# Other durations and the shared port in an attention planner, and float64 weights decoded by a multiplication

## The chip, the cores and the metric

The kernel runs on one core of one Trainium2 chip. The metric is the time of one execution on the device in microseconds. Its engines are named as the profile names them: PE (TensorE, matrix products), DVE (VectorE), ACT (ScalarE), POOL (GpSimd) and SP, whose queue issues the DMAs.

## The reference

Three layers follow one another: attention in which a query sees only the keys that fall in the same hash bucket, a dense layer pair with the Mish activation, and eight experts with a gate that is normalised by eight Sinkhorn rounds.

```python
q_bits = (np.einsum('bhsd,dk->bhsk', q, proj) > 0).astype(np.int64)   # 16 heads, 768 tokens, 64 wide
...
mask = q_bucket[:, :, :, None] == k_bucket[:, :, None, :]
scores = np.where(mask, scale * np.matmul(q, k.transpose(0, 1, 3, 2)), -1000000000.0)
scores = scores - np.max(scores, axis=-1, keepdims=True)
attn = np.exp(scores) / (np.sum(np.exp(scores), axis=-1, keepdims=True) + 1e-09)
x = np.matmul(attn, v)                                                # -> 1536 tokens x 512
...
h = x @ w_in                                                          # 512 x 2048, w_in and w_out are float64
x = (h * np.tanh(np.log1p(np.exp(h)))) @ w_out
...
for e in range(8):                                                    # P: the normalised gate
    out += P[:, e:e + 1] * (np.maximum(x @ w1[e], 0.0) @ w2[e])
```

`w_in` and `w_out` reach the kernel as 64-bit words and are turned into pairs of 32-bit parts on the chip.

## The kernel before

Attention comes first (to 291.3 us of the profiled execution), then the dense layer and the experts, which are one long row of matmuls.

Attention works on 32 units `u`, half a head's 384 queries each, and six blocks `c` of 128 keys. Scores are computed twice. `s_mm` (L379) makes them with the queries on the partitions, rounded, only for the row maxima: `s_max` (L393, DVE, read from PSUM; one buffer, tag `s`), `cols` (L398, L399, DVE) gathers three maxima and flags into columns, `rows_mm` (L412, PE) transposes them, `rows_cp` (L421, ACT) copies them out, and three small DMAs (`rows_move`) put them under the queries. `st_mm` (L429, L430) then makes the exact scores with the keys on the partitions and the maximum already subtracted; `st_exp` (L435, ACT) takes the exponential into one of five buffers `p`. Blocks 0, 1, 3 and 4 are split into a rounded part (`split_hi`, the tile `ph`, L438) and a rest (`split_lo`, the tile `plo`, L441, POOL) for three fast products; blocks 2 and 5 go into one slow product as they are. Both are `av_mm` (L479). `av_out` (L487 on DVE, L489 on ACT) reads the result out, `norm` (L498 to L510, and casts and subtractions on L438 and L441) divides.

For each head, `prep_hi` (L300, ACT) and `prep_lo` (the tile `lo`, L441) split the loaded queries and keys, `bits_mm` and `bits_cmp` (L326 to L338) make the hash bits, `split_v` (the tiles `vh`, `vl`) splits the values, and `vsum_red` (L348, DVE) sums them.

Beside all this, eight half chunks of the 64-bit weights are loaded and decoded while attention runs (`decode`, L132 to L165). A half chunk is 128 x 512 numbers, each a low and a high 32-bit word. Parts 0, 1 and 3 to 6 work on the high word: the sign is kept aside (L135), the absolute value is taken (L137 on DVE or L139 on ACT), it is clamped (L143), its exponent is moved into the 32-bit place (L147), the sign comes back (L151), and the power of two is cut out (L155). Part 2 (L141, ACT) turns the low word into a float, part 7 (L157, POOL) scales it and part 8 (L159) adds the two. `weight_hi` and `weight_lo` (L171, L176) split the finished chunk. The other 24 half chunks are decoded beside the dense layer by the same function, in an order written out in the code.

What sets the order inside attention is a list scheduler that runs while the program is built. Every step is a task with an engine (or a choice of two), a cost in us, a due time in steps and the tasks it waits for. In each round the planner takes, of the tasks whose predecessors are placed, the one with the smallest start plus 0.012 times its due time on each engine, and of these the earliest start. `free[e]` is when an engine is free, `ends[k]` when a task's readers may start. So a cost changes the order in which instructions stand in each engine's queue; at run time each queue is worked in that order, with semaphores for the data.

```python
task("P1.8|D.87" if h else "D.5|", 0, due - 14.0 + 1 if h else -50, prep_lo, h, i, after=[his[i], *moved])
task("D", 0.87, due + 2 * t + 0.5, s_max, u, t, after=[nm(s_mm, u, t)] + [nm(cols, u - 2)] * (t == 0 and u > 1))
...
free[e] = start + cost
ends[k] = start + cost + LAT[e]
```

Of the kernel before, what the change touches and what calls it, by code (L numbers as in the profile page):

```python
# [22 lines left out]
E = 8  # L23
# [16 lines left out]
RECEIPT = 0.95  # L40
# [6 lines left out]
LOW64 = float(2.0 ** -15)  # L47
HIGH64 = float(122880.0)
# [9 lines left out]
def lsh_attention_moe_kernel(  # L58
# [72 lines left out]
    def decode(i, j, part, e="A"):  # L131
        t = staged[i, j]  # L132
        lw, hw = t[:, :, 0], t[:, :, 1]
        if part == 0:
            nc.vector.tensor_scalar(out=sgn[j], in0=hw, scalar1=-0x80000000, scalar2=None, op0=ALU.bitwise_and)  # L135
        elif part == 1 and e == "D":
            nc.vector.tensor_scalar(out=hw, in0=hw, scalar1=0x7FFFFFFF, scalar2=None, op0=ALU.bitwise_and)  # L137
        elif part == 1:
            nc.scalar.activation(f32(hw), f32(hw), AF.Abs)  # L139
        elif part == 2:  # L140
            nc.scalar.activation(f32(lw), lw.bitcast(U32), AF.Copy, scale=2.0 ** -52)  # L141
        elif part == 3:
            nc.vector.tensor_scalar(  # L143
                out=f32(hw), in0=f32(hw), scalar1=LOW64, scalar2=HIGH64, op0=ALU.max, op1=ALU.min
            )
        elif part == 4:
            nc.vector.tensor_scalar(  # L147
                out=hw, in0=hw, scalar1=0x38000000, scalar2=3, op0=ALU.bitwise_xor, op1=ALU.logical_shift_left
            )
        elif part == 5:  # L150
            nc.vector.scalar_tensor_tensor(  # L151
                out=hw, in0=hw, scalar=0x7FFFFFFF, in1=sgn[j], op0=ALU.bitwise_and, op1=ALU.bitwise_or
            )
        elif part == 6:
            nc.vector.tensor_scalar(out=sgn[j], in0=hw, scalar1=-0x800000, scalar2=None, op0=ALU.bitwise_and)  # L155
        elif part == 7:
# [26 lines left out]
    def attention():  # L183
        with ExitStack() as a:
# [334 lines left out]
            def task(engine, cost, due, f, *args, after=(), lag=None, ring=None, frees=None):  # L519
                tasks[f.__name__, *args] = (engine, cost, due, f, args, list(after), lag, ring, frees)  # L520

            LAT = {"E": 0.2, "A": 0.12, "D": 0.1, "P": 0.12, "Q": 0.0}
# [11 lines left out]
            task("D", 1.4, -99, clear_start)  # L534
            task("E", 5.0, -99, warm_up, after=[nm(clear_start)])
            task("A", 1.5, -99, load_table, after=[nm(clear_start)])
            for j in range(4):
                task("Q", 0.6, (-98, -97, -26, 20)[j], load_const, j, lag=0.1)
            task("D", 0.55, -8, proj_parts, after=[nm(clear_start), nm(load_const, 0)])
            for c in range(2):  # L540
                task("D", 0.2, -2, count_rows, c, after=[nm(load_const, 2), nm(clear_start)])
            task("D", 0.3, 20, gate_parts, after=[nm(load_const, 3)])
            for i in range(NS):
                for n, kind in enumerate(("sq", "bk", "one")):
                    e = "D" if (kind, i) in FAST else "P"
                    task(e, 0.7, -8.5 + 3 * i + n / 4, clear, kind, i, after=[nm(clear, "bk", i)] * (n == 2))
            for i in range(2):
                for kind in ("vt", "vh", "vl"):
                    task("P", 0.35, -3 + 2 * i, clear, kind, i)


            for h in range(NH):
# [5 lines left out]
                task("Q", 0.6 if h else 1.2, due - 24 if h else -99, load_qk, h, lag=1.65 if h else 1.3,  # L558
# [3 lines left out]
                for i in range(len(halves(h))):  # L562
                    task("A", 0.75 if h else 0.38, due - 14.0 if h else -50, prep_hi, h, i,
                         after=[nm(load_qk, h), *moved] + [nm(bits_mm, h - 1, j) for j in range(2) if h])
                    task("P1.8|D.87" if h else "D.5|", 0, due - 14.0 + 1 if h else -50, prep_lo, h, i, after=[his[i], *moved])
# [739 lines left out]
```

## Time and profile before

| | us |
|---|---|
| median of 3 runs | 1586.91 (1584.88 to 1586.96) |
| the profiled execution | 1585.57 |
| its span, first to last instruction | 1583.8 |
| attention, to the first matmul of the dense layer | 291.3 |
| PE busy, whole span | 1549.1 (98%) |
| in attention, busy: PE, DVE, POOL, ACT | 261.8, 251.8, 204.0, 186.3 |

A busy time is the sum of the spans in which an engine had an instruction under way. On PE these overlap and their ends are modelled, so the number of matmuls in a stretch says more than the busy time. On DVE and POOL an instruction's span includes time in which it stood still.

### The profile page before, as it was taken

The page shows a single profiled execution, that of the slowest core. Times are in us where ns is not written, and L with a number is a line of the kernel's source. Part 1 is how long each engine was busy: PE and PEld are TensorE (multiplying, and loading weights), DVE is VectorE, ACT ScalarE, POOL GpSimd, SP SyncE. Part 2 cuts the span into 40 slices and gives each one's busy share as a digit, 9 for nine tenths or more (in the row PEclk, how much of TensorE's full clock was granted, in tenths as well). Part 3 has the DMA queues.
Part 4 walks back from the last instruction along what each step waited for, and adds up shares of the span by engine and source line. Part 5 has one row for each costly group of instructions (what it writes and reads, how often), then busy time and mean ns, then how long its engine had stood idle before and what let it go on. Part 6 is the DMA issues. An engine that isn't in the chain of part 4 may idle for free.

```text
span 1583.8 us, 20022 instructions
## 1 busy us (share of the span) xinstructions
PE 1549.1 (98%) x7439; PEld 1350.0 (85%) x7439; DVE 851.2 (54%) x1462; ACT 623.6 (39%) x1131; POOL 866.4 (55%) x706
## 2 busy tenths in 40 slices
PE   7898999999999999999999999999999999999999
PEld 5687888888888878889989999899998989989997
DVE  7999998587883222665333425455534243334343
ACT  4566766643333322223333333333333333333331
POOL 5677677433333340226666666666666656565652
PEclk9999999999999999999999999999999999999999
DMA  6644552021212010002222222222232222222221
GB/s 153 166 136 111 138 138 52 28 80 54 76 57 80 0 54 0 17 30 62 76 61 77 60 74 62 72 67 67 76 98 67 67 67 67 67 67 67 67 67 41
DMA packets 62641, 113.44 MB, mean 72 GB/s; under 512 B 18176, under 2 KB 18920, under 8 KB 62544
## 3 DMA queue, kind: packets, MB, share of 16 engines
q1 hardware_dynamic: 62544, 112.17, 24.4%
q8 instruction: 59, 0.97, 0.2%
q14 instruction: 38, 0.31, 0.1%
HBM read 89.22 MB, written 3.15 MB: 58 GB/s over the span
## 4 chain that ended last, share of the span: by engine, by line
PE 87%; DVE 9%; issue 2%; POOL 1%; ACT 1%; DMA 0%; DVEq 0%; ACTq 0%
PE y L1179 29%; PE u L1116 26%; PE y L817 12%; PE h L781 4%; PE h L783 4%; PE h L782 4%; PE pav L479 3%; DVE mx L393 3%; PE ps L379 1%; PE pst L430 1%; PE pst L429 1%; DVE ph L438 1%; DVE vs L348 1%; DVE xu L510 1%; POOL plo L441 0%
## 5 line engine op out<-in xcount | busy, mean ns | idle before, releaser
L1179 PE MATMUL y<-w,gh 128*128 128x512 f32 x672 | 218.5, 393 | 0.0
L1179 PE MATMUL y<-ww,gh 128*128 128x512 f32 x672 | 218.1, 393 | 0.0
L1124 ACT ACTIVATE gh<-c 128x384 fp32r<-128x384 f32 x168 | 88.0, 526 | 278.4 <-DVE c L1136 278.4
L441 POOL TENSOR_TENSOR plo<-p,ph 128x384 fp32r<-128x384 f32 x128 | 141.0, 1110 | 63.9 <-ACT ph L438 33.3
L1179 PEld LDWEIGHTS y<-ww,gh 128*128 128x128 f32 x672 | 124.8, 188 | 18.1
L1179 PEld LDWEIGHTS y<-w,gh 128*128 128x128 f32 x672 | 124.8, 188 | 17.8
L1005 POOL TENSOR_TENSOR w<-stage,w 128x1024 fp32r<-128x1024 f32 x28 | 67.1, 2396 | 132.4 <-ACT w L1001 132.4
L1005 POOL TENSOR_TENSOR ww<-stage,ww 128x1024 fp32r<-128x1024 f32 x28 | 67.1, 2395 | 126.8 <-ACT ww L1001 126.8
L1179 PE MATMUL y<-w,gl 128*128 128x512 f32 x336 | 132.2, 394 | 0.0
L1179 PE MATMUL y<-ww,gl 128*128 128x512 f32 x336 | 132.2, 393 | 0.0
L998 POOL TENSOR_TENSOR w<-sraw,w 128x1024 fp32r<-128x1024 f32 x28 | 67.3, 2405 | 107.3 <-ACT w L994 107.3
L157 POOL TENSOR_TENSOR stage<-stage,sgn 128x512 f32<-128x512 f32 x32 | 45.7, 1428 | 120.2 <-DVE sgn L155 48.8
L817 PE MATMUL y<-gh,w 128*128 128x512 f32 x336 | 110.2, 389 | 0.0
L1136 DVE TENSOR_TENSOR u<-u,p 128x384 f32<-128x384 f32 x56 | 31.2, 557 | 146.2 <-PE u L1116 146.2
L435 ACT ACTIVATE p<-pst 128x384 f32<-128x384 f32 x192 | 92.4, 487 | 39.8 <-PE pst L430 36.3
L781 PE MATMUL h<-xh,w 128*128 128x512 f32 x252 | 99.5, 395 | 0.0
L783 PE MATMUL h<-xh,w 128*128 128x512 f32 x252 | 98.3, 390 | 0.4 <-POOL w L176 0.4
L782 PE MATMUL h<-xl,w 128*128 128x512 f32 x252 | 98.2, 390 | 0.0
L1129 DVE SCALAR_TENSOR_TENSOR gl<-c,gh 128x384 fp32r<-128x384 f32 x168 | 94.3, 561 | 6.0 <-ACT gh L1124 0.2
L393 DVE TENSOR_REDUCE mx<-ps 128x1 f32<-128x768 f32 x95 | 89.9, 946 | 13.2 <-PE ps L379 12.7
L1124 ACT ACTIVATE gh<-u 128x384 fp32r<-128x384 f32 x56 | 27.6, 492 | 161.9 <-PE u L1116 161.9
L1129 DVE SCALAR_TENSOR_TENSOR gl<-u,gh 128x384 fp32r<-128x384 f32 x56 | 31.2, 557 | 110.1 <-ACT gh L1124 110.1
(247 smaller groups left out, 4032.7 us busy)
## 6 DMA issues: line engine op xcount, KB each, us to landing
stage<-in_w_dram SPq DMA_DIRECT2D x152, 512.0 KB
raw<-in_qk_dram SPq DMA_DIRECT2D x13, 384.0 KB
wx<-hi SPq DMA_DIRECT2D x20, 192.0 KB
vt<-in_v_dram SPq DMA_DIRECT2D x16, 192.0 KB
out_dram<-acc SPq DMA_DIRECT2D x12, 256.0 KB
zq<-hi SPq DMA_DIRECT2D x11, 192.0 KB
ak<-hi SPq DMA_DIRECT2D x11, 192.0 KB
zq<-lo SPq DMA_DIRECT2D x11, 192.0 KB
```

The source lines that it names most:

```text
L393: nc.vector.tensor_reduce(out=m[:, t, 0:1], in_=s_t[t][:, :, :HALF], axis=AX.XY, op=ALU.max, negate=True)
L435: nc.scalar.activation(p_t[u, c], st_t.pop((u, c))[:, :HALF], AF.Exp, scale=0.125)
L441: (nc.gpsimd if e == "P" else nc.vector).tensor_sub(out, in0, in1)
L781: nc.tensor.matmul(t, wt[:, 0, f], xh[:, kc, c], start=(kc == 0), stop=False)
L782: nc.tensor.matmul(t, wt[:, 0, f], xl[:, kc, c], start=False, stop=False)
L783: nc.tensor.matmul(t, wt[:, 1, f], xh[:, kc, c], start=False, stop=(kc == KC - 1))
L817: nc.tensor.matmul(yps[j], x, y, start=(head and m == 0), stop=(tail and m == 2))
L1005: nc.gpsimd.tensor_sub(y[:, 1, :], t, f32(y)[:, 0, :])
L1116: nc.tensor.matmul(bank[x], weight(u, a, m, kc), moving(u, b, mm, kc), start=(first and n == 0), stop=(n == 5), skip_group_check=not first)
L1124: nc.scalar.activation(hi, src, AF.Relu)
L1129: nc.vector.scalar_tensor_tensor(out=lo, in0=src, scalar=0.0, in1=f32(hid_u[u, c][0]), op0=ALU.max, op1=ALU.subtract)
L1179: nc.tensor.matmul(y_t[t], (hi, hi, lo)[m][:, t % 3 * P:(t % 3 + 1) * P], y, start=(k == 0 and first and m == 0), stop=(k == NF // 2 - 1 a ...
```

## The change

- **Decoding.** ScalarE multiplies the high word, read as a 32-bit float, by 2^-112 (part 0), which moves the exponent and keeps the sign. The sign extraction, the absolute value and the exclusive-or go; the clamp is symmetric, and the shift writes the scratch tile. Nine parts become eight; two of them are on ACT, where one or two were. The same function serves the 24 half chunks beside the dense layer.
- **Costs.** A task's cost is now looked up by engine and function. The new numbers are durations, and a separate table `OVER` says how much of it the next instruction on that engine overlaps, `SEEN` how long after the end a reader may start. For the unsplit `av_mm` the cost goes from 0.65 to 0.36, with 0.5 us until its reader; a DMA's receipt from 0.95 to 1.6.
- **The shared port.** The planner keeps, for DVE and POOL, until when each holds the port that they share. A DVE task of the set `SHARED` starts no earlier than POOL's hold ends less 0.13 us, a POOL task no earlier than DVE's.
- `split_v`, `prep_lo`, `split_hi` and the last decode part still have a choice of two engines, now at the new costs.

```diff
-RECEIPT = 0.95
+RECEIPT = 1.6
...
-    def decode(i, j, part, e="A"):
+    def decode(i, j, part, e="P"):
...
         if part == 0:
-            nc.vector.tensor_scalar(out=sgn[j], in0=hw, scalar1=-0x80000000, scalar2=None, op0=ALU.bitwise_and)
-        elif part == 1 and e == "D":
-            nc.vector.tensor_scalar(out=hw, in0=hw, scalar1=0x7FFFFFFF, scalar2=None, op0=ALU.bitwise_and)
+            nc.scalar.activation(f32(hw), f32(hw), AF.Copy, scale=SCALE64)
         elif part == 1:
-            nc.scalar.activation(f32(hw), f32(hw), AF.Abs)
+            nc.scalar.activation(f32(lw), lw.bitcast(U32), AF.Copy, scale=2.0 ** -52)
         elif part == 2:
-            nc.scalar.activation(f32(lw), lw.bitcast(U32), AF.Copy, scale=2.0 ** -52)
+            nc.vector.tensor_scalar(out=f32(hw), in0=f32(hw), scalar1=HIGH64, scalar2=-HIGH64, op0=ALU.min, op1=ALU.max)
         elif part == 3:
-            nc.vector.tensor_scalar(
-                out=f32(hw), in0=f32(hw), scalar1=LOW64, scalar2=HIGH64, op0=ALU.max, op1=ALU.min
-            )
+            nc.vector.tensor_scalar(out=sgn[j], in0=hw, scalar1=3, scalar2=None, op0=ALU.logical_shift_left)
...
+            COST = {
+                "E": dict(warm_up=3.6, bits_mm=0.53, s_mm=0.355, rows_mm=0.2, st_mm=0.355, av_count=0.18, vsum_mm=0.3),
...
+            SHARED = {prep_lo, cols, split_hi, split_v, decode, clear, clear_start, count_rows, gate_parts}
+            OVER = {"E": 0.0, "A": 0.09, "D": 0.09, "P": 0.04}
+            SEEN = {"E": 0.2, "A": 0.05, "D": 0.05, "P": 0.06}
+            HELD = 0.13
...
-                    task("P1.8|D.87" if h else "D.5|", 0, due - 14.0 + 1 if h else -50, prep_lo, h, i, after=[his[i], *moved])
+                    task("PD" if h else "D", due - 14.0 + 1 if h else -50, prep_lo, h, i, cost=None if h else 0.6, after=[his[i], *moved])
...
-                    task("E", 0.5 if sp else 0.65, i + 1.0, av_mm, u, c,
+                    task("E", i + 1.0, av_mm, u, c, cost=0.53 if sp else 0.36,
...
+                real = r
+                if e == "D" and shares(k):
+                    real = max(r, held["P"] - HELD)
+                elif e == "P":
+                    real = max(r, held["D"])
+                return r, real
...
+                    end = real + cost
+                    if f is cols:
+                        end = max(end, start + 2 * cost, held["P"] - HELD + cost)
+                    if e == "P" or e == "D" and shares(k):
+                        held[e] = end - (0.05 if e == "D" else 0.0)
+                    free[e] = end - OVER[e]
+                    ends[k] = end + (0.5 if f is av_mm and args[1] not in SPLIT else SEEN[e])
...
-                for part, lag in enumerate((0, 0, 0, 0, 0, 0.5, 0.5, 0.5, 1.4)):
+                for part, lag in enumerate((0, 0, 0, 0, 0.5, 0.5, 0.5, 1.4)):
```

How the order moves at three places. In the changed kernel's rows the line numbers are its own: `s_max` is L385, `cols` L390 and L391, the clamp L139, the shift L141, the `or` L143, the cut L147.

VectorE at the start of attention, before the change: the hash bits of head 0 (`sq`, `bk`), the gate weights (`wgr`), the first maxima (`mx`) and the first `cols`. Here `mx_142` belongs to even units and `mx_143` to odd ones.

```order
L338 TENSOR_SCALAR bk_127<-pbits,cst 12x384
L292 CAST wgr<-wg 128x4x8
L293 TENSOR_TENSOR wgr<-wg,wgr 128x4x8
L393 TENSOR_REDUCE mx_142<-ps 128x1
L388 TENSOR_REDUCE mx_142<-ps 128x1 x2
L391 TENSOR_TENSOR mx_142<-mx_142 128x1
L393 TENSOR_REDUCE mx_142<-ps 128x1
L398 TENSOR_REDUCE col<-mx_142 128x3
L399 TENSOR_SCALAR col<-mx_142 128x3x3
L393 TENSOR_REDUCE mx_143<-ps 128x1
```

The gate weights stand ahead of the first maximum here, and the first `cols` ahead of the next unit's maximum. The same place in the changed kernel:

```order
L330 TENSOR_SCALAR bk_127<-pbits,cst 12x384
L277 TENSOR_SCALAR vf<-ones,idt 4x2x64 x2
L385 TENSOR_REDUCE mx_142<-ps 128x1
L380 TENSOR_REDUCE mx_142<-ps 128x1 x2
L383 TENSOR_TENSOR mx_142<-mx_142 128x1
L385 TENSOR_REDUCE mx_142<-ps 128x1
L385 TENSOR_REDUCE mx_143<-ps 128x1
L390 TENSOR_REDUCE col<-mx_142 128x3
L391 TENSOR_SCALAR col<-mx_142 128x3x3
```

The gate weights are gone from this place, the count rows (`vf`) have taken it, and the next unit's maximum stands ahead of `cols`.

VectorE at the second half chunk of the weights (the scratch tile `sgn_87`), before the change:

```order
L441 TENSOR_TENSOR xl<-xu,xh 128x384
L135 TENSOR_SCALAR sgn_87<-stage 128x512
L441 TENSOR_TENSOR vl_133<-vt_129,vh_131 128x4x64
L137 TENSOR_SCALAR stage<-stage 128x512
L143 TENSOR_SCALAR stage<-stage 128x512
L147 TENSOR_SCALAR stage<-stage 128x512
L151 SCALAR_TENSOR_TENSOR stage<-stage,sgn_87 128x512
L393 TENSOR_REDUCE mx_142<-ps 128x1
```

Five decode operations stand between two maxima. The same half chunk in the changed kernel:

```order
L385 TENSOR_REDUCE mx_142<-ps 128x1
L141 TENSOR_SCALAR sgn_87<-stage 128x512
L385 TENSOR_REDUCE mx_142<-ps 128x1
L390 TENSOR_REDUCE col<-mx_142 128x3
L391 TENSOR_SCALAR col<-mx_142 128x3x3
L495 RECIPROCAL nr<-nr 128x12
L479 STREAM_TRANSPOSE rs<-pav 64x384
L497 STREAM_TRANSPOSE rs<-nr 128x384
L385 TENSOR_REDUCE mx_143<-ps 128x1
L502 TENSOR_TENSOR xu<-xu,rs 128x384
L385 TENSOR_REDUCE mx_143<-ps 128x1
L143 SCALAR_TENSOR_TENSOR stage<-stage,sgn_87 128x512
```

Each decode operation now has a maximum behind it, and the half chunk is spread over two units.

GpSimd between the first two half chunks (`stage<-stage,sgn` is decode's product, `plo` is `split_lo`, `lo` is `prep_lo`), before the change:

```order
L157 TENSOR_TENSOR stage<-stage,sgn_86 128x512
L159 TENSOR_TENSOR dec_82<-stage 128x512
L498 TENSOR_SCALAR nr<-rs 128x12
L441 TENSOR_TENSOR plo<-p,ph 128x384
L441 TENSOR_TENSOR lo<-raw,hi 128x768
L441 TENSOR_TENSOR plo<-p,ph 128x384 x7
```

And in the changed kernel:

```order
L433 TENSOR_TENSOR lo<-raw,hi 128x768
L433 TENSOR_TENSOR plo<-p,ph 128x384 x4
L149 TENSOR_TENSOR stage<-stage,sgn_86 128x512
L433 TENSOR_TENSOR plo<-p,ph 128x384
L433 TENSOR_TENSOR lo<-raw,hi 128x768
L433 TENSOR_TENSOR plo<-p,ph 128x384 x2
L151 TENSOR_TENSOR dec_82<-stage 128x512
L433 TENSOR_TENSOR plo<-p,ph 128x384 x3
```

Two of the large subtractions `lo` stand around the first product here, where one did; over all of attention GpSimd has 11 of `lo<-raw,hi` instead of 3, and DVE 2 instead of 10 (with `lo<-rs,hi` moved the other way, a net 7).

## Rows read from the trace of the kernel before

**Rows 1.** Stages of attention: stretch, its length, busy us (instructions) by engine, clock.

```profile
core 0: us, PE busy (x) PEld busy (x) DVE busy (x) ACT busy (x) POOL busy (x), PEclk, DMA share, GB/s
...
40.00:160.00 120.00, 106.62 (x522) 90.93 (x520) 112.67 (x183) 77.91 (x171) 87.57 (x77) 0.97 0.52 138
160.00:240.00 80.00, 75.31 (x391) 66.41 (x390) 75.88 (x132) 54.80 (x120) 57.07 (x55) 1.00 0.50 134
...
260.00:291.30 31.30, 30.42 (x157) 26.52 (x155) 17.50 (x33) 21.89 (x49) 22.89 (x24) 1.00 0.00 1
```

**Rows 2.** The same view, a stretch of the dense layer with decoding beside it.

```profile
331.00:351.00 20.00, 20.00 (x90) 16.57 (x89) 15.96 (x26) 9.43 (x16) 7.21 (x5) 1.00 0.24 79
```

**Rows 3.** Waits, 20 to 291.3 us: waiter, releaser: us in total, times, longest.

```profile
PE prow L412 <- DVE col L399: 14.4, 14, 2.1
...
PE ps L379 <- DVE mx L393: 2.5, 4, 1.2
ACT p L435 <- POOL plo L441: 2.4, 4, 0.9
```

**Rows 4.** Timeline, 82 to 89 us: start, us, instruction, [idle before, releaser].

```profile
82.25 2.39 POOL L176 TENSOR_TENSOR w<-dec,w 128x1024 fp32r<-128x1024 f32 x1
83.11 1.82 DVE L137 TENSOR_SCALAR stage<-stage 128x512 int32<-128x512 int32 x1
...
84.96 1.12 DVE L143 TENSOR_SCALAR stage<-stage 128x512 f32<-128x512 f32 x1
...
86.11 1.11 DVE L147 TENSOR_SCALAR stage<-stage 128x512 int32<-128x512 int32 x1
87.13 0.94 DVE L393 TENSOR_REDUCE mx<-ps 128x1 f32<-128x768 f32 x1
...
88.41 0.28 PE L412 MATMUL prow<-idt,col 128*12 128x128 f32 x1 [2.05 <-DVE col L399]
```

**Rows 5.** Line 137 alone: count, shortest, median and longest in ns, starts.

```profile
L137 DVE TENSOR_SCALAR stage<-stage x3: 409/427/1819, 45.2 to 83.1; 128x512 int32<-128x512 int32 x3
```

**Rows 6.** Timeline of VectorE, 12 to 18 us.

```profile
12.08 1.43 DVE L292 CAST wgr<-wg 128x32 fp32r<-128x32 f32 x1
...
16.90 0.16 DVE L399 TENSOR_SCALAR col<-mx 128x9 f32<-128x9 f32 x1
17.89 0.96 DVE L393 TENSOR_REDUCE mx<-ps 128x1 f32<-128x768 f32 x1 [0.83 <-PE ps L379]
```

**Rows 7.** Timeline, 127 to 131 us.

```profile
127.76 2.34 POOL L176 TENSOR_TENSOR w<-dec,w 128x1024 fp32r<-128x1024 f32 x1
...
127.91 2.23 DVE L399 TENSOR_SCALAR col<-mx 128x9 f32<-128x9 f32 x1
...
130.19 0.28 PE L412 MATMUL prow<-idt,col 128*12 128x128 f32 x1 [2.11 <-DVE col L399]
```

**Rows 8.** VectorE by shape, to 291.3 us: count, busy us, mean ns, idle before.

```profile
L438 DVE CAST ph<-p 128x384 fp32r<-128x384 f32 x38 | 18.2, 478 | 2.0 <-ACT p L435 1.5
...
L441 DVE TENSOR_TENSOR lo<-raw,hi 128x768 fp32r<-128x768 f32 x10 | 10.2, 1021 | 1.8 <-ACT hi L300 1.7
...
L135 DVE TENSOR_SCALAR sgn<-stage 128x512 int32<-128x512 int32 x8 | 4.6, 572 | 0.0
...
L438 DVE CAST vh<-vt 128x256 fp32r<-128x256 f32 x7 | 2.1, 306 | 0.0
```

**Rows 9.** GpSimd by shape, to 291.3 us.

```profile
L441 POOL TENSOR_TENSOR plo<-p,ph 128x384 fp32r<-128x384 f32 x128 | 141.0, 1110 | 63.9 <-ACT ph L438 33.3 <-DVE ph L438 30.1
...
L441 POOL TENSOR_TENSOR vl<-vt,vh 128x256 fp32r<-128x256 f32 x11 | 10.0, 912 | 5.7 <-DVE vh L438 5.7
...
L441 POOL TENSOR_TENSOR lo<-raw,hi 128x768 fp32r<-128x768 f32 x3 | 5.8, 1950 | 0.0
```

**Rows 10.** Timeline of PE, 287 to 288 us, around an unsplit product.

```profile
287.15 0.81 PE L479 MATMUL pav<-p,vt 128*128 128x384 f32 x2
287.50 0.63 PE L429 MATMUL pst<-zq,ak 128*128 128x384 f32 x1
287.97 0.34 PE L430 MATMUL pst<-sq,bk 100*128 100x384 f32 x1
```

More of the change, by code (lines that the diff above doesn't have):

```diff
@@ L667, in attention @@
                     }[part]
-                    task(e, cost, due + 0.3 * part, decode, i, j, part, after=after)
+                    task(e, due + 0.3 * part, decode, i, j, part, after=after, cost=cost)
                 if j == 1 and i < RING_A + NX:
                     last = 2 * (NH - 3 + i - RING_A) + 1
-                    task("A", 0.95, due + 5, weight_hi, i, after=[nm(decode, i, x, 8) for x in range(2)] + ([nm(weight_lo, i - 1)] if i else [])
+                    task("A", due + 5, weight_hi, i, after=[nm(decode, i, x, 7) for x in range(2)] + ([nm(weight_lo, i - 1)] if i else [])
@@ L715, in attention @@
-                    if cand:
-                        x = min(cand, key=lambda c: c[0] + DELTA * c[1])
-                        if best is None or x[0] < best[0]:
-                            best = (*x, e)
-                start, _, k, e = best
-                engine, cost, due, f, args, after, lag, ring, frees = tasks[k]
-                options = dict(choices(tasks[k]))
-                for x in options:
-                    todo[x].remove(k)
-                cost = options[e]
-                free[e] = start + cost
@@ L726, in attention @@
-                ends[k] = start + cost + LAT[e]
-                if lag:
-                    bus = max(start + cost + 0.5, bus) + lag
-                    ends[k] = bus + RECEIPT
+                    cand = [(b[1] + DELTA * tasks[k][2], k, b) for k in ks for b in [begin(e, k)] if b]
+                    if cand:
+                        _, k, b = min(cand, key=lambda c: c[0])
+                        if best is None or b[0] < best[1][0]:
+                            best = k, b, e
+                k, (start, real), e = best
@@ new lines, in attention @@
+                engines, cost, due, f, args, after, lag, ring, frees = tasks[k]
+                for x in engines:
+                    todo[x].remove(k)
+                if isinstance(cost, dict):
+                    cost = cost[e]
+                if e == "Q":
+                    free[e] = start + (cost or 0.6)
+                    bus = max(free[e] + 0.5, bus) + lag
+                    ends[k] = bus + RECEIPT
+                else:
+                    if cost is None:
+                        cost = COST[e][f.__name__]
+                    end = real + cost
[5 more added lines that the diff above has]
+                    ends[k] = end + (0.5 if f is av_mm and args[1] not in SPLIT else SEEN[e])
```

165 lines of the change are left out of this document (86 added, 79 removed).

## Prediction

> **What bounds the kernel now.** I read the busy times by stage first, then who PE waited for, then VectorE's and GpSimd's rows around the longest of those waits, and last the groups by shape that the change moves. The stages [rows 1]: from 291.3 us on, the expert layers run, and PE is busy for all of each 20 us there [rows 2]. Nothing that this change touches can shorten them, so a gain must come out of the 291.3 us of attention. There the reader is to compare two stretches that do the same kind of work. Between 40 and 160 us PE issues 522 matmuls in 120 us, 4.35 per us; between 160 and 240 us it issues 391 in 80, 4.89 per us. VectorE is busy 94% and 95% of them. The closing stretch, with VectorE at 56%, issues 5.02 per us. So attention can go faster than 4.35, and the tuned order itself does so for 80 us.
>
> The waits say what is in the way: PE waited 14.4 us, in 14 pieces of up to 2.1 us, for the transposed row maxima because `cols` on VectorE was late, and 2.5 us for `s_max` to free the one score buffer [rows 3]. The wait that ends at 88.41 us shows how this comes about [rows 4]. VectorE ran three decode operations in a row, of 1.82, 1.12 and 1.11 us, before the maximum that `cols` needs. The first is long: the shortest of its line is 0.41 us [rows 5]. It ended at 84.93, when GpSimd's 2.39 us weight split had just ended (84.64). The one that ends at 130.19 us is plainer: `cols`, 0.16 us elsewhere [rows 6], took 2.23 us beside a GpSimd operation of 2.34 us [rows 7]. VectorE operations on SBUF thus stand still while GpSimd works, and the maxima, which read PSUM, keep their 0.94 to 0.96 us [rows 4, 6]. The Trainium skill, page "SBUF — State Buffer", section "Who interferes with whom", calls the port pair of the two an exclusive lock on which the later one fully blocks; the trace agrees, with the 2.23 us.
>
> **What the change takes off VectorE.** Counts are from the built order of both kernels, durations are means [rows 5, 8].
> - Decoding, 8 half chunks in attention: the sign extraction goes (8 x 0.572 = 4.6 us), and the three absolute values that VectorE made go (0.409 + 0.427 + 1.819 = 2.7). The other four keep their kind and number; one loses its second operation.
> - `split_hi`: 38 casts become 22 (16 x 0.478 = 7.6). `split_v`'s first part: 7 become 0 (7 x 0.306 = 2.1).
> - `prep_lo`: 10 of the large subtractions become 3 (7 x 1.021 = 7.1).
>
> Together 24.1 us of the 206.1 us that VectorE is busy in the three stretches of [rows 1]; four small subtractions, one chunk sum and one output split go the same way and are not counted.
>
> **What it puts elsewhere.** ScalarE gets three more decode passes, 16 casts and 7 splits. It was busy 154.6 of those 231.3 us [rows 1], so 77 us are free, and no long wait of PE's names it; I cost this at nothing. If that cover were gone, each cast in front of an exponential would cost PE its half microsecond. GpSimd gets 7 large subtractions at 1.95 us (13.7) and 4 small ones at 0.91 (3.6) [rows 9]: 17.3 us. It stood idle 63.9 us before the `split_lo` operations, waiting for ScalarE or VectorE [rows 9]. But a 1.95 us operation queues ahead of the next `split_lo`, for which PE's product and, through the five buffers, the exponentials wait. Bounds: nothing (all within the idle time) to 13.7 us (each in PE's way). The nearest row is the exponentials' wait for `split_lo`, 2.4 us in all [rows 3], so I take +2.
>
> In the expert layers 24 half chunks move one pass each to ScalarE and take two off VectorE. ScalarE is busy 9.4 of 20 us there and PE has no gap [rows 2]: nothing. The code order there puts both ScalarE passes ahead of the activation, as one stood before; PE works several steps ahead of it.
>
> **The start.** The gate weights' conversion (1.43 us, with a second operation behind it) stood ahead of the first maximum and moves behind it; the count rows take its place. That is about 1 us earlier. But the first `cols` now stands behind the first maximum of the next unit, which ran at 17.89 us, 0.99 us after `cols` [rows 6]. Between -1 and +1; I take 0.
>
> **What the new order is worth.** The order shows the decoding of the second half chunk, five operations ahead of a maximum before, now with maxima between them. The new planner also charges a VectorE operation that shares with GpSimd the time until the other ends, so it should keep `cols` away from a 2.3 us weight split. Two ways to size it:
> - By rate: if 40 to 160 us ran at the 4.89 per us of the next stretch, 522 matmuls would take 106.8 us: -13.2.
> - By waits: PE's waits for `cols` and `s_max` are 16.9 us, and the low clock after the long ones (0.97 granted over those 120 us [rows 1], full rate being 2.4 GHz and the lower level 1.2) is worth 3.6: 20.5. Two thirds of that is 13.7.
>
> I take the rate, since the same planner reached it with the old costs at an equally busy VectorE. The stretch from 160 us on I leave as it is: PE idles little there. The sum is -13.2 + 2 + 0 = -11.2 us. Against the profiled execution, 1585.57 us with a span of 1583.8, that is 1574.4, a span of 1572.6. The median of the runs lies 1.34 us above the profiled one, so the predicted time is 1586.9 - 11.2 = 1575.7.
>
> **Rivals.**
> - *The gain is held by the shared port* (0.23). If the pair of VectorE and GpSimd is what is full, moving work between them frees nothing. Here: the casts and decode operations that leave the pair free 17.0 us (7.6 + 2.1 + 4.6 + 2.7), of which about half is waiting (the shortest absolute value is 0.41 us of a mean of 0.89), so some 9; `prep_lo` gives back 7.1 and takes 13.7, and GpSimd's small ones 3.6 against what they saved. That leaves about -4 us: 1583, between -7 and +1. For it: the long VectorE rows. Against it: GpSimd's 63.9 us of idle time, and the planner's aim at the few operations that stand on PE's path. The Trainium skill, page "Perfetto Trace Analysis", section "Optimizing Scalar/DVE Operations", says that offloading between those two "might not help"; by that rule this is the outcome.
> - *Slower: the planner misjudges the unsplit product* (0.09). It now charges `av_mm` of an unsplit chunk 0.36 us of PE, where before it charged 0.65. In the trace the matmul after such a pair begins 0.35 us later by its row, but that row lasts 0.63 us where the next one lasts 0.34 [rows 10]: it stood 0.29 us longer, and the pair holds PE some 0.65 us. 64 of them are 64 x 0.29 = 18.6 us of PE work that the plan doesn't see. Exponentials and casts are then queued as if their scores came earlier, and other work waits behind them. From 11.2 of the 18.6 us exposed the change loses; all exposed would be 1586.9 - 11.2 + 18.6 = 1594. Against it: PE's own order hardly depends on it, and each unit's maxima tie the engines together again.
> - *Nearly all the waiting goes* (0.08): -20.5, and the start its best, -1: 1565.
> - *The new costs change the order but not the waits* (0.04): VectorE is relieved, yet `s_max`, the single score buffer and `cols` stay a chain of the same length: 1586.
>
> **How the numbers follow.** My forecast, 1575.7, has 0.56. Its own range is 1570 to 1581.5: at the low end the waits' sizing with the start's -1 and the stretch of 160 to 240 us at the closing 5.02 per us (391 in 77.9 us, -2.1), at the high end half of GpSimd's bound, 6.9, and the start's +1. What a measurement of this kernel can tell from no change is 0.2%, 3.2 us: below 1583.7 is faster, above 1590.1 slower. Faster: 0.56 + 0.08 + 0.13 of the port's 0.23 = 0.77. Same: 0.10 of the port's and 0.04 = 0.14. Slower: 0.09. Eight in ten lie between 1567 and 1585.5: 0.04 below, about 0.15 above.
>
> **What would show it.** Right: the first expert matmul starts near 280 us; the 40 to 160 us stretch holds over 560 matmuls; PE's wait for `cols` falls below 6 us; VectorE's busy share between 40 and 240 us falls from 94% to about 82%. The port would show as GpSimd busier, with VectorE's casts and decode operations still twice their shortest. The slower rival would show as ScalarE and VectorE idle before exponentials and maxima while their scores are still in PE's queue. Wrong would be PE waiting for `split_lo` by over 8 us, or any gap in the expert layers.

## The result and the profile after

| | before | after |
|---|---|---|
| median (runs) | 1586.93 (4) | 1572.43 (4) |
| ratio, 95% interval | | 0.9909, 0.9889 to 0.993 |
| the profiled execution, its span | 1585.57, 1583.8 | 1572.67, 1570.8 |
| first matmul of the dense layer | 291.28 | 278.17 |
| span from there on | 1292.5 | 1292.6 |

The kernel became 14.5 us faster, 12.9 between the two profiled executions. In these two, all of it lies ahead of the first dense matmul. The stretch of the dense layer that answers to [rows 2] (40 us after its first matmul) holds the same 90 matmuls with PE busy throughout, though VectorE fell from 15.96 to 10.54 us:

```profile
317.90:337.90 20.00, 20.00 (x90) 16.57 (x89) 10.54 (x19) 10.86 (x18) 6.94 (x4) 1.00 0.23 79
```

The stages of attention in the changed kernel, with the columns of [rows 1]: stretch, length, busy us (instructions) of PE, PEld, DVE, ACT and POOL, PE's clock.

```profile
0.00:40.00 40.00, 31.36 (x121) 24.26 (x121) 32.87 (x60) 17.93 (x36) 22.23 (x32) 0.83 0.64 156
40.00:160.00 120.00, 115.08 (x593) 101.10 (x594) 103.72 (x172) 92.61 (x207) 98.29 (x92) 1.00 0.59 152
160.00:240.00 80.00, 76.99 (x388) 67.91 (x387) 67.70 (x113) 57.23 (x131) 63.55 (x62) 0.96 0.50 130
240.00:278.10 38.10, 35.59 (x177) 30.32 (x177) 23.05 (x40) 25.57 (x58) 29.15 (x29) 1.00 0.05 15
```

Two stretches of the kernel before that are not in [rows 1], its start and its end:

```profile
0.00:40.00 40.00, 30.05 (x115) 23.40 (x116) 30.59 (x58) 17.40 (x34) 22.24 (x32) 1.00 0.65 154
240.00:291.20 51.20, 49.73 (x254) 43.46 (x253) 32.61 (x58) 36.19 (x81) 37.14 (x38) 1.00 0.14 36
```

Between 40 and 160 us PE issued 593 matmuls instead of 522: 4.94 per us against 4.35. The next 80 us hold as many as before (388 against 391). The end lost a little: 177 in 38.1 us, 4.65 per us, where before issued 254 between 240.0 and 291.2, 4.96 per us. PE's granted clock rose from 0.97 to 1.00 between 40 and 160 us, but fell from 1.00 to 0.96 in the next 80 us and from 1.00 to 0.83 in the first 40.

The waits, 20 us to the end of attention: waiter, releaser: us in total, times, longest. They answer to [rows 3].

```profile
ACT p L427 <- POOL plo L433: 11.4, 15, 1.8
PE prow L404 <- DVE col L391: 5.4, 6, 2.3
PE pst L421 <- ACT p L427: 1.9, 3, 1.1
PE ps L371 <- DVE mx L385: 0.2, 1, 0.2
```

PE's wait for `cols` fell from 14.4 to 5.4 us and the one for `s_max` from 2.5 to 0.2. The exponentials' wait for `split_lo` rose from 2.4 to 11.4.

VectorE and GpSimd by shape, to 278.1 us: count, busy us, mean ns, idle before. They answer to [rows 8, 9].

```profile
L391 DVE TENSOR_SCALAR col<-mx 128x9 f32<-128x9 f32 x32 | 16.7, 521 | 0.0
L430 DVE CAST ph<-p 128x384 fp32r<-128x384 f32 x22 | 11.5, 521 | 5.3 <-ACT p L427 2.2 <-ACT xh L430 1.3 <-PE pav L471 1.1
...
L433 DVE TENSOR_TENSOR lo<-raw,hi 128x768 fp32r<-128x768 f32 x2 | 1.9, 943 | 0.0
```

```profile
L433 POOL TENSOR_TENSOR plo<-p,ph 128x384 fp32r<-128x384 f32 x128 | 136.6, 1079 | 41.5 <-ACT ph L430 30.9 <-DVE ph L430 7.7 <-PE pst L421 1.1
L433 POOL TENSOR_TENSOR lo<-raw,hi 128x768 fp32r<-128x768 f32 x11 | 20.5, 1860 | 0.4 <-ACT hi L292 0.4
```

The first row is the surprise: `cols` did not get shorter. Its second operation takes 0.521 us on average where it took 0.355 before, and it still stands still beside GpSimd. Timeline of three engines around 148 us: start, us, instruction, [idle before, releaser]:

```profile
147.88 2.36 POOL L168 TENSOR_TENSOR w<-dec,w 128x1024 fp32r<-128x1024 f32 x1
...
148.55 1.72 DVE L391 TENSOR_SCALAR col<-mx 128x9 f32<-128x9 f32 x1
...
150.41 0.27 PE L404 MATMUL prow<-idt,col 128*12 128x128 f32 x1 [1.16 <-DVE col L391]
```

`cols` ends at 150.27, 0.03 us after the weight split. So the stalls are there as before, but PE loses less to them. Why, the runs below were to tell.

### The profile page after: what moved, and what is told of

Its sections match the earlier page's. It is cut to its first block, busy times and chain, and to the rows that moved or that the text cites. A ratio compares the mean times of both kernels' runs of the same rounds, so it can differ in the third digit from the quotient of the medians.

```text
span 1570.8 us, 20028 instructions
## 1 busy us (share of the span) xinstructions
PE 1546.4 (98%) x7439; PEld 1349.5 (86%) x7439; DVE 798.1 (51%) x1367; ACT 644.2 (41%) x1181; POOL 874.3 (56%) x719
## 3 DMA queue, kind: packets, MB, share of 16 engines
q1 hardware_dynamic: 62544, 112.17, 24.4%
## 4 chain that ended last, share of the span: by engine, by line
PE 92%; DVE 4%; POOL 1%; issue 1%; DMA 1%; ACT 1%; SPq 0%; ACTq 0%; POOLq 0%; DVEq 0%
PE y L1206 30%; PE u L1143 26%; PE y L844 12%; PE pav L471 5%; PE h L808 4%; PE h L810 4%; PE h L809 4%; PE ps L371 2%; PE pst L421 2%; PE pst L422 2%; DVE mx L385 1%; POOL plo L433 1%; DVE col L391 1%; PE lg L870 0%; DMA stage<-in_w_dram 0%
## 5 line engine op out<-in xcount | busy, mean ns | idle before, releaser
L433 POOL TENSOR_TENSOR plo<-p,ph 128x384 fp32r<-128x384 f32 x128 | 136.6, 1079 | 41.5 <-ACT ph L430 30.9
L385 DVE TENSOR_REDUCE mx<-ps 128x1 f32<-128x768 f32 x95 | 90.3, 950 | 25.3 <-PE ps L371 24.6
```

The lines of the kernel that those rows point to most:

```text
L385: nc.vector.tensor_reduce(out=m[:, t, 0:1], in_=s_t[t][:, :, :HALF], axis=AX.XY, op=ALU.max, negate=True)
L433: (nc.gpsimd if e == "P" else nc.vector).tensor_sub(out, in0, in1)
```

## The experiments

The theory: the planner's new rule of the shared port keeps maxima and `cols` from being queued late, and that is most of the gain. The rivals: the cheaper decoding does it by relieving VectorE; the new durations alone do it; any other order would have moved the time as much. Beside the times I read one number worked out from the timelines of PE and VectorE: how long after the end of its scores each of the 95 large maxima of `s_max` started, on average.

| kernel | us | ratio to before, interval | first dense matmul | PE's waits for `cols` L404 / `s_max` | maxima late by |
|---|---|---|---|---|---|
| before | 1586.9 | | 291.3 | 14.4 / 2.5 | 0.56 |
| new decoding alone (e1) | 1582.5 | 0.9975 (0.9965–0.9985) | 288.3 | 13.7 / 3.0 | 0.55 |
| no port rule (e3) | 1577.7 | 0.9947 (0.9934–0.996) | 283.0 | 7.3 / 10.2 | 0.57 |
| no port rule, product 0.65 (e9) | 1581.2 | 0.9968 (0.9956–0.9981) | 285.5 | 12.1 / 7.3 | 0.60 |
| no port rule, `lo` on VectorE (e13) | 1578.0 | 0.9949 (0.9936–0.9962) | 286.8 | 9.1 / 6.2 | 0.57 |
| before, `lo` on GpSimd (e8) | 1589.8 | 1.002 (1.0011–1.0029) | 296.5 | 15.6 / 10.7 | 0.62 |
| **changed kernel** | 1572.4 | 0.9909 (0.9889–0.993) | 278.2 | 5.4 / 0.2 | 0.28 |
| due times at 0.013 (e6) | 1570.2 | 0.9902 (0.9886–0.9917) | 275.4 | 4.2 / 0.2 | 0.27 |
| old decoding (e2) | 1571.9 | 0.991 (0.9895–0.9925) | 278.1 | 2.5 / 3.3 | 0.34 |
| product 0.65 (e4) | 1563.2 | 0.9854 (0.984–0.9867) | 269.4 | 2.0 / 0.9 | 0.37 |
| product 0.65, 0.013 (e10) | 1565.9 | 0.9875 (0.9862–0.9889) | 273.5 | 1.0 / 0.7 | 0.33 |
| `lo` on VectorE (e5) | 1562.1 | 0.9851 (0.9837–0.9864) | 267.9 | 0.8 / 1.5 | 0.25 |
| product 0.65, `lo` on VectorE (e11) | 1565.4 | 0.9871 (0.9858–0.9885) | 274.1 | 1.7 / 1.9 | 0.30 |
| product 0.65, `lo` on GpSimd (e12) | 1566.0 | 0.9875 (0.9862–0.9889) | 272.1 | 3.3 / 2.6 | 0.36 |

The first six kernels plan without the port rule (before, e1 and e8 with the old durations too), the last eight with it. The two groups overlap in neither the time nor the lateness of the maxima. Each ratio is against the runs of before on the same chip, whose medians were 1585.9 to 1586.9 us.

**The decoding alone (e1).** The kernel before with `decode` and its tasks in eight parts, at costs 0.67 (ScalarE, twice), 0.35, 0.35, 0.7, 0.4, 1.25 and the choice at the end as it was.

```diff
...
-            nc.vector.tensor_scalar(out=sgn[j], in0=hw, scalar1=-0x80000000, scalar2=None, op0=ALU.bitwise_and)
...
+            nc.scalar.activation(f32(hw), f32(hw), AF.Copy, scale=SCALE64)
...
```

> The kernel before with the new decoding alone: the planner, its old cost table and its old rule stay, only the decode tasks get the costs of the eight parts. Theory (the planner's order keeps the transposed maxima early, and that is the gain): VectorE loses 4.6 us of sign extractions and 2.7 us of absolute values in attention, but PE still waits over 10 us for cols (14.4 before, 5.4 in the changed kernel), the first dense matmul stays after 286 us (291.3 before, 278.2 after), and the time falls by at most 4 us: 1583 to 1587. Rival (the relief of VectorE is the gain, whoever orders it): 7.3 us less on VectorE, each microsecond of it worth about half of one to PE as in the whole change (24 us off, 14.5 gained), and the first dense matmul near 287, with PE's wait for cols falling in proportion, to some 10 us: about 1582.5. Beside the dense layer nothing moves in either: the span after the first dense matmul stays 1292.5 us.

The time is the rival's, 0.25% or some 4 us off; after the first dense matmul the span is 1292.5 us as before. But PE's waits are the theory's, they did not fall:

```profile
PE prow L404 <- DVE col L391: 13.7, 18, 2.4
...
PE ps L371 <- DVE mx L385: 3.0, 4, 1.1
```

So the cheaper decoding is worth some 4 us under the old planner, a good quarter of the whole gain. It isn't what removed the waits.

**The planner alone (e2).** The changed kernel with the old nine parts.

```diff
...
-                costs = (("A", None), ("A", None), ("D", None), ("D", None), ("D", 0.68), ("D", None), ("P", None), ("DP", {"D": 0.68, "P": 1.04}))
...
+                costs = (("D", None), ("AD", {"A": 0.68, "D": 0.41}), ("A", None), ("D", None), ("D", None), ("D", 0.68), ("D", None), ("P", None), ("DP", {"D": 0.68, "P": 1.04}))
...
```

> The changed kernel with the old decoding in nine parts, at the durations of the trace (0.41 on VectorE, 0.68 on ScalarE), so the new planner and costs alone. Theory: most of the gain stays. VectorE has the 7.3 us of attention more; at half a microsecond of PE each that is 3 to 4 us: 1573 to 1578, the first dense matmul at 278 to 283 us, PE's wait for cols below 8 us. Rival (relief of VectorE by the multiplication counts most): 1580 or more, first dense matmul after 286, the waits for cols back above 10 us.

1571.9 us, just under the theory's range: even the 3 to 4 us that I gave the decoding are not to be seen here. Under the new planner the nine parts cost nothing that can be measured. So the relief of VectorE paid under the old planner (one pair) and not under the new one (one pair); why was not tried.

**Without the port rule (e3).**

```diff
-                if e == "D" and shares(k):
-                    real = max(r, held["P"] - HELD)
-                elif e == "P":
-                    real = max(r, held["D"])
...
-                        end = max(end, start + 2 * cost, held["P"] - HELD + cost)
+                        end = start + 2 * cost
```

> The changed kernel whose planner does not count the shared port: costs, overlaps and decoding as changed, but a VectorE task no longer waits in the plan for GpSimd's hold, nor the other way round. Theory (the port model is what keeps cols away from long GpSimd operations): cols again falls beside weight splits and products of over 1 us, its 128x9 row's mean rises from 0.52 us towards 0.8 or more, PE's wait for cols rises from 5.4 to 10 us or more, and the time is 1577 to 1583. Rival (durations alone are the gain): within 3 us of the changed kernel, 1570 to 1575, PE's wait for cols as there.

The time held: 1577.7 us, 5.3 above the changed kernel. The mechanism as I had put it did not. `cols` got shorter, 0.399 us on average, not longer, and PE's wait for it rose to 7.3 us, not to 10 or more. PE instead waited for the score buffer that `s_max` frees:

```profile
PE ps L371 <- DVE mx L385: 10.2, 14, 1.0
PE prow L404 <- DVE col L391: 7.3, 13, 1.2
```

So the rule doesn't keep small operations away from GpSimd's long ones. It charges VectorE's shared operations the time until GpSimd's end, and the plan then doesn't queue as many operations ahead of a maximum. That is what the last column of the table shows: 0.57 us late without the rule, 0.28 with it. In the timelines, two or more VectorE operations stood between the end of the scores and the maximum at 31 of the 95 maxima in e3, and at 14 in the changed kernel. Whether it must be the port's rule, or whether a plain surcharge on the same operations would do, no run tells.

In the change itself the rule is thus 5.3 us, not most of the 14.5: without it e3 is already 8.5 us faster than before. That did not come from a shorter sum of waits. In e3 PE waits 17.5 us for `cols` and `s_max` together (before: 16.9), and the maxima are as late as before. The trace shows where it lies. The first 40 us hold 127 matmuls instead of 115, and those from 40 to 160 us 550 instead of 522. In the second stretch the granted clock is 1.00 instead of 0.97, and the longest of these waits is 1.2 us, where it was 2.1. At most two decode operations stand between two maxima, where five did. That fits the picture of long waits with a low clock behind them, but no run tested the new durations by themselves.

```profile
0.00:40.00 40.00, 30.92 (x127) 25.01 (x128) 33.87 (x64) 19.34 (x39) 18.90 (x30) 0.83 0.73 175
40.00:160.00 120.00, 108.09 (x550) 93.13 (x550) 116.04 (x191) 81.93 (x180) 86.16 (x78) 1.00 0.51 136
```

**Without the rule, at two other settings (e9, e13).** The same edit, with `cost=0.53 if sp else 0.65` for `av_mm`, and with `prep_lo` on `"D"` alone:

> Both single edits together: no shared port in the plan, and the unsplit av_mm charged 0.65 us. It is the second pair for each. With the port rule and 0.65 the time was 1563.2, without it and with 0.36 it was 1577.7, with it and 0.36 1572.4. Theory (two separate effects that add): 1577.7 - 9.2 = 1568.5, between 1566 and 1571, PE's wait for cols and for s_max's buffer together over 8 us (17.5 without the rule, 5.6 with it). Rival (the cost of 0.65 alone does it, the port rule matters only where PE is misjudged): 1562 to 1565, with those waits under 5 us. Rival (neither is an effect, only other orders): 1573 or more.

> The changed kernel without the port rule in the plan and with the large subtractions on VectorE: the third pair for the port rule, at one and the same place for these operations (1562.1 with the rule). The pairs so far: 5.3 us (with 11 subtractions on GpSimd against 4) and 18.0 us (5 against 11). Theory (the rule keeps cols and s_max early and is worth some 10 us by itself): 1569 to 1577, PE's waits for cols and s_max together over 10 us (2.2 with the rule). Rival (what the rule did was to move subtractions between the engines): 1560 to 1566, those waits under 5 us.

1581.2 and 1578.0 us, where the same settings with the rule give 1563.2 and 1562.1. Three pairs thus put the rule at 5.3, 18.0 and 15.9 us.

In the third pair the engine of the large subtractions is fixed, so the rule didn't act by moving those. My sum for the second pair (two effects that add, 1568.5) was 12.7 us too low, and the time fell where the last rival had it (neither is an effect, 1573 or more). Against that rival, for the port rule, stand three differences of one sign and the lateness of the maxima; for the product's cost it isn't refuted. e13 lies 1 us above the theory's range.

**A control (e6).** `DELTA = 0.013` for 0.012, the weight of the due times.

> The changed kernel with the planner's weight of the due times at 0.013 in place of 0.012, no duration or rule changed: a control that tells how much an arbitrary other order of the same planner moves the time. If the differences between kernels of a few us are to be read as the effect of a rule, this one stays within 3 us of the changed kernel: 1569.5 to 1575.5, first dense matmul at 275 to 281 us, PE's wait for cols 3 to 8 us. If it moves by 5 us or more either way, a single comparison of two planners says nothing below that, and the effects of the port rule (5.3 us between the changed kernel and the one without it) and of the unsplit product's cost (9.2 us) need their second pair.

1570.2 us; its interval overlaps that of the changed kernel. As a control it fails its purpose: by the two traces, with buffer numbers left out, 6 lines of PE's 1276 differ from the changed kernel's and none of GpSimd's. It is nearly the same kernel run again, 2.2 us faster, and says nothing of what another order of the same planner costs.

**The unsplit product at 0.65 us (e4, e10).** This tests the slower rival of the prediction.

```diff
-                    task("E", i + 1.0, av_mm, u, c, cost=0.53 if sp else 0.36,
+                    task("E", i + 1.0, av_mm, u, c, cost=0.53 if sp else 0.65,
```

> The changed kernel with the unsplit av_mm charged 0.65 us as before, in place of 0.36 (its reader is still planned 0.5 us behind it). 64 of them: the plan is 18.6 us longer on PE than with 0.36. If the plan with 0.36 hides PE work that matters, the plan with 0.65 is nearer to the machine and the time falls: by up to a third of the 12 us that PE still waits, 1568 to 1571, with fewer waits of the exponentials for split_lo (11.4 us in the changed kernel). If, as predicted, PE's own order hardly depends on it, the time is within 3 us of the changed kernel, 1570 to 1575, with the first dense matmul between 276 and 281 us.

1563.2 us, 9.2 below the changed kernel, more than I had thought possible. By the traces 442 lines of PE's order differ from the changed kernel's, so it does depend on that cost. The rate held through the stretch that the change had left alone (413 matmuls in it against 388), and the end ran without a gap:

```profile
160.00:240.00 80.00, 78.72 (x413) 70.53 (x413) 72.91 (x124) 59.27 (x133) 61.88 (x62) 1.00 0.49 129
240.00:269.30 29.30, 29.30 (x150) 25.74 (x149) 16.08 (x33) 21.30 (x48) 22.68 (x24) 1.00 0.06 20
```

The same edit with the due times at 0.013:

> The unsplit av_mm charged 0.65 us, with the weight of the due times at 0.013: the second pair for that cost, against the changed kernel at 0.013. Theory (charging what PE really does lets the plan place exponentials, casts and subtractions where they are needed): again 6 to 12 us faster than the pair with 0.36, 1560 to 1567, PE idle in attention after 20 us under 9 us (11.3 in the changed kernel, 7.4 with 0.65). Rival (the 9.2 us were the luck of one order): within 4 us of the pair with 0.36, 1569 or more.

1565.9 against 1570.2: 4.3 us, less than the 6 to 12 expected, with PE idle for 10.1 us where I had expected under 9. It stands 2.7 us above the run at 0.012, with 90 lines of difference on PE; differences of that size between two orders I don't read further. Since e6 has nearly the changed kernel's order, the two comparisons share their slower side.

**The large subtractions on VectorE (e5), and what lies behind it (e11, e12, e8).**

```diff
-                    task("PD" if h else "D", due - 14.0 + 1 if h else -50, prep_lo, h, i, cost=None if h else 0.6, after=[his[i], *moved])
+                    task("D", due - 14.0 + 1 if h else -50, prep_lo, h, i, cost=None if h else 0.6, after=[his[i], *moved])
```

> The changed kernel with all large subtractions of prep_lo (11 on GpSimd, 2 on VectorE in it) forced onto VectorE, under the same planner and costs. It prices the work that the change put on GpSimd. As predicted (+2 us for GpSimd's extra work, 7.1 us of relief on VectorE): 11 x 1.02 us go back to VectorE, at half a microsecond of PE each that is 5 us lost against 2 to 4 us won on GpSimd: 1573 to 1578, with the waits of the exponentials for split_lo falling from 11.4 us to under 6. Rival (the shared port holds what moves between the two, so it doesn't matter which of them does it): within 2.5 us of the changed kernel, 1570 to 1575, whatever the waits. Rival (GpSimd is now the one that is late; its subtractions cost PE what they last): faster by 4 us or more, under 1568.5.

1562.1 us, 10.3 below the changed kernel: the GpSimd rival's outcome. The exponentials' wait and the stretch from 160 us:

```profile
ACT p L427 <- POOL plo L433: 1.6, 3, 0.8
```

```profile
160.00:240.00 80.00, 79.61 (x418) 71.33 (x416) 72.04 (x125) 61.08 (x138) 63.15 (x64) 1.00 0.48 128
```

But the run with 0.65 had only 5 of these subtractions on GpSimd, the changed kernel 11. Both edits might have acted through the same operations. Three runs tell: both edits together, the cost with all of the subtractions on GpSimd, and the kernel before with them there.

> The changed kernel with both edits that were faster: unsplit av_mm charged 0.65 us and prep_lo's large subtractions on VectorE. Alone they gave 1563.2 and 1562.1. The run with 0.65 had 5 of the subtractions on GpSimd where the changed kernel has 11, the one with 0.65 and another weight of the due times 6. Theory (the cost acts by its own, by placing exponentials and casts rightly): the two add in part, 1553 to 1559. Rival (the cost of 0.65 acted because the planner then put fewer subtractions on GpSimd): no more than the better one alone, 1560 to 1564.

> The changed kernel with unsplit av_mm charged 0.65 us and the large subtractions forced onto GpSimd (13 there, 11 in the changed kernel, 5 in the run with 0.65 alone). Theory (the cost acts by its own): 3 to 7 us of its 9.2 stay, 1565 to 1570. Rival (it acted through fewer subtractions on GpSimd, at some 0.9 us each: 10.3 us by 11): 1572 to 1576, with the exponentials' wait for split_lo over 9 us (5.3 with 0.65 alone, 11.4 in the changed kernel).

> The kernel before with the large subtractions of prep_lo (10 on VectorE, 3 on GpSimd in it) forced onto GpSimd under the old planner. It prices the move from the other side: does a large subtraction on GpSimd cost PE time wherever it stands? Theory (GpSimd is late in front of split_lo when it holds these 1.9 us operations, as the run with all of them on VectorE showed, 10 us faster than the changed kernel): slower than before by 2 to 10 us, 1588 to 1596, with the exponentials' wait for split_lo up from 2.4 us to over 6. Rival (in the old order VectorE is the late one, so 10 us of relief there wins): 1578 to 1584, PE's wait for cols under 12 us, split_lo's wait unchanged.

The edits don't add: 1565.4 is above either of them alone, and above both ranges of that expectation. With 13 subtractions on GpSimd the kernel at 0.65 still runs in 1566.0 us, within the theory's range. So at 0.65 the number of subtractions on GpSimd isn't the cause either: none, 5 and 13 of them give 1565.4, 1563.2 and 1566.0. What goes with the time better is how long the exponentials wait for `split_lo`: 11.1 to 12.0 us in the three slow kernels with the rule (the changed one, e6 and e2), 1.6 to 9.5 in the five fast ones. With 13 there, at 0.65:

```profile
ACT p L427 <- POOL plo L433: 3.9, 6, 1.5
```

In the kernel before, moving ten subtractions to GpSimd cost 3 us, within the theory's range; the wait that grew was the one for `s_max`, from 2.5 to 10.7 us, while the one for `split_lo` reached only 4.9 where the theory had asked for over 6.

**One place in the trace.** About half of what separates the changed kernel from e4 and e5 lies at one place. Between 175 and 185 us it issues 30 matmuls, where the ten microseconds before 170 and after 185 hold 57 each; the 27 that are missing are some 5 us. Its timeline, and below it the two stretches, with the columns of [rows 1]:

```profile
173.85 0.49 ACT L427 ACTIVATE p<-pst 128x384 f32<-128x384 f32 x1 [1.67 <-POOL plo L433]
175.78 1.80 POOL L433 TENSOR_TENSOR lo<-raw,hi 128x768 fp32r<-128x768 f32 x1
175.88 0.58 DVE L479 STREAM_TRANSPOSE rs<-pav 64x384 f32<-64x384 f32 x1 [1.54 <-ACT xu L481]
176.43 1.18 DVE L391 TENSOR_SCALAR col<-mx 128x9 f32<-128x9 f32 x1
177.66 0.38 PE L404 MATMUL prow<-idt,col 128*12 128x128 f32 x1 [2.29 <-DVE col L391]
```

```profile
175.00:180.00 5.00, 2.71 (x9) 1.78 (x8) 3.29 (x6) 1.98 (x5) 4.32 (x4) 0.60 0.40 119
180.00:185.00 5.00, 5.00 (x21) 4.73 (x21) 1.29 (x2) 2.70 (x6) 2.06 (x3) 0.71 0.26 79
```

An exponential waits 1.67 us for `split_lo`. ScalarE's read-out (`xu`) comes late behind it, and VectorE's waits for that one with `cols` queued behind. `cols` then stands still beside a large subtraction on GpSimd. PE waits 2.29 us, and after that its granted clock is 0.60 and 0.71 for two stretches of 5 us. e6, of nearly the same order, has the same place (2.31 us at 174.99); in e4 and e5 PE waits nowhere longer than 1.0 us after 50 us. Of the clock: the one execution of the changed kernel with 1.000 granted took 1569.3 us, those with 0.992 and 0.993 took 1572.2 to 1575.0.

**What stays open.** The rest of why the changed kernel's own setting (0.36, free choice) is 6 to 10 us slower than five neighbours, and why their orders avoid that place. Two edits each mend it, but neither gains in every setting: 0.65 gained 9.2 and 4.3 us with the free choice, but lost 3.3 with the subtractions on VectorE and 3.5 without the port rule. Of the 3.3 one wait is visible, 4.0 us of PE for the small DMA that puts the maxima under the queries (`sq<-row`) at 67.2 us in e11; why that DMA came late wasn't tried. `lo` on VectorE (e5) and the product at 0.65 (e4) both beat both kernels; e5's 1562.1 us is 1.5% under before.

## Why the prediction was right

The median came out 3.3 us under the forecast and inside the range. Step by step:

- **Where the gain lies: right.** 13.1 us in attention, none in the expert layers.
- **What VectorE sheds: right.** I counted 24.1 us; its busy time in attention fell from 251.8 to 227.4, by 24.4. Between 40 and 240 us it fell to 86% (103.72 + 67.70 of 200) and not to 82%: 17.1 of the 24.4 us lie in that stretch.
- **The new order, -13.2: right in place and size.** I took the rate 4.89 per us for 40 to 160 us; it was 4.94, and the waits for `cols` and `s_max` fell from 16.9 to 5.6 us. Over 560 matmuls were to stand there; it is 593. The 71 more are 14.3 us at the 4.96 per us of before's last stretch. The granted clock there, 0.97 before, is 1.00.
- **How the new order does it: half right.** I had the port rule keeping `cols` away from 2.3 us weight splits. It still runs beside them ([rows 7] has 2.23 us, the row at 148.55 us above 1.72). The rule pays because maxima come earlier. And the rule that I named is 5.3 us here: without it the new costs and the decoding together still gave 8.5 us against before, at the same waits. So the size of 13.2 is right in sum, but more of it came with the durations and the decoding than with the rule; in e3 the longest of these waits and the low clock went while their sum stayed.
- **The start and ScalarE, 0: near enough.** The first 40 us hold 6 matmuls more, 1.2 us. PE's waits for the exponentials rose from 0.5 to 1.9 us. With 0.6 us for three matmuls fewer between 160 and 240 us and the 2.4 us of the next point that makes -14.3 - 1.2 + 0.6 + 2.4 = -12.5, of the 13.1 that the first dense matmul shows; the stages' counts sum to 1282 before and 1279 after, which is the other 0.6.
- **GpSimd, +2: the term that was mis-sized.** At the end of attention a loss of 2.4 us shows (177 matmuls would take 35.7 us at before's 4.96 per us, and took 38.1); that it is GpSimd's is not shown. But e5, where the order changes along with them, shows that this kernel is 10.3 us slower with its subtractions where the plan put them, inside the bounds of 0 to 13.7 and far from 2. The row I took, 2.4 us of waits for `split_lo`, was one of a kernel with three such operations, and the wait became 11.4. The announced sign, PE itself waiting for `split_lo` by over 8 us, did not appear (1.0 us): at the place shown above the cost went through an exponential, `cols` and the clock.
- **160 to 240 us left alone, 0: right by luck** (388 matmuls against 391). The place at 177.66 us lies in it and costs some 27 matmuls; without it the stretch would have gained. In e4 and e5, which lack that place, it holds 413 and 418.
- **The port rival (1583): wrong in time, and its sign half there.** GpSimd did get busier (204.0 to 213.2 us in attention). The casts kept their length (0.478 to 0.521 us), the clamp did not (0.794 us on average before, 0.486 after, by shape), and the work moved between the two engines did change the time. The Trainium skill, page "Perfetto Trace Analysis", section "Optimizing Scalar/DVE Operations", has it that offloading between them might not help. The runs show both: at 0.65 the place of 13 subtractions makes under 3 us, in the changed kernel 10.3.
- **The slower rival: its mechanism is not dead.** I held against it that PE's order hardly depends on the product's cost; it does. Charging 0.65 gained 9.2 us here, though with the opposite sign in two other settings. It reduced the gain at most and never came near a loss against before.
- **The two others.** Nearly all waiting gone (1565) was not reached by the change, but by its neighbours e4 and e5. An order that changes nothing (1586) fell.
- **The range's low end** leaves GpSimd's +2 out without saying so: 13.7 + 1 + 2.1 us below 1586.9 is 1570.1; with the +2 it is 1572.1, and the result still lies inside.
- **A reading that was too wide:** that VectorE's operations on SBUF stand still while GpSimd works. In the trace of [rows 7] the first operation of `cols`, which reads and writes SBUF too, took its usual 0.16 us beside the same weight split; the second one stood still.

## What to carry to other kernels

When a planner sets the order, a duration that is wrong by contention can be worth correcting even if the contention itself stays: the stalls of `cols` got longer here and PE waited less. Judge a planner's edit by several settings, not by one pair: the port rule gave 5 to 18 us in three pairs, always the same sign, while charging the product 0.65 changed the time by between -9 and +4 us. When work is moved to an engine that has idle time, look at what stands behind it in that queue: GpSimd had 63.9 us of idle time before `split_lo`, yet in the changed order the exponentials' wait went from 2.4 to 11.4 us, while in another order thirteen of the same operations left it at 3.9.

## What the runs showed of the hardware

A VectorE operation of 128 x 9 elements, 0.16 us alone, took 2.23 us before and 1.72 us after beside a GpSimd operation of 2.34 and 2.36 us, and ended within 0.1 us of it both times; the longest after, 1.82 us at 110.88 us, ended 0.02 us after a large subtraction of 1.82 us on GpSimd. A reduction to 128 x 3, which in the kernel before ran ahead of it beside the same GpSimd operation, kept its length:

```profile
127.83 0.16 DVE L398 TENSOR_REDUCE col<-mx 128x3 f32<-128x6 f32 x1
```

The maxima, which read PSUM, took 0.946 and 0.950 us on average in the two kernels, and none of the 190 took more than 0.96. The large subtraction took 1.84 to 1.95 us on average on GpSimd in these kernels, and 0.94 to 1.35 us on VectorE. The longest average is e4's, whose three longest (1.83, 1.84 and 2.04 us) ran beside GpSimd operations of 1.0 us and more, the others 0.94 to 1.12:

```profile
L433 DVE TENSOR_TENSOR lo<-raw,hi 128x768 fp32r<-128x768 f32 x8 | 10.8, 1348 | 0.0
```

After PE's wait of 2.29 us that ends at 177.66 us in the changed kernel, at a granted clock of 0.60 and 0.71 over the next two stretches of 5 us, matmuls began 0.32 us apart instead of 0.18.
